# The scaling step of the float64 weight conversion: 60 of 60 on ScalarE in the first feed-forward, where it was 24 of 60

## The chip, the cores and the metric

The kernel runs on one core of one Trainium2 chip. The core has five engines that run side by side, each through its own queue in order: TensorE (PE in the profile; PEld is its weight load), VectorE (DVE), ScalarE (ACT), GpSimd (POOL) and SyncE (SP), which here issues the DMAs. Engines wait for one another by semaphores. The metric is the device time of one execution in microseconds (us), as the median of several runs; lower is better.

## The reference, cut to what matters

```python
x = attention(q, k, v, M_prev, z_prev, beta)   # 4 batches, 8 heads, 576 rows, 64 columns
x = x.reshape(2304, 512)                       # 4 batches of 576 tokens
a = x @ w1                                     # 512 x 1024
b = x @ w2                                     # 512 x 1024
h = a * b @ w3                                 # 1024 x 1024
x = h @ w_out                                  # 1024 x 512
gate = 1 / (1 + exp(-(x @ w_gate)))            # 512 x 1536
val = x @ w_val                                # 512 x 1536
return gate * val @ w_out2                     # 1536 x 512
```

All of attention's inputs are float32. The weights are float64, and the kernel gets them as the bits of 64-bit integers; turning them into float32 is part of the time. The product w3 @ w_out is computed first and once, so that the first feed-forward is (a * b) @ (w3 @ w_out).

## The kernel before, in words

**Stages.** The four batches are worked through one after the other. `ffn(b)` is the feed-forward of batch b, and beside it the attention of batch b + 1 runs in slices that `drive` hands out. Ahead of `ffn(0)` a stage `start()` runs the attention of batch 0 and the first half of w3 @ w_out (PSUM tile `wps`, functions `prep` and `prep_units`). Within a feed-forward PE computes `ab` (x @ w1 and x @ w2, 8 blocks of columns), `xw` (times w3 @ w_out, 4 blocks), `gv` (x @ w_gate and x @ w_val, 12 blocks f = 0 to 11) and `ot` (times the last weight, 4 blocks). Each product is made of three fp32r matmuls, high times high, low times high and high times low, in `prod`, so each weight is split in a high and a low half by `split_rows` (line 311 casts on ACT, line 313 subtracts on DVE or POOL).

**Weights.** Only up to the end of batch 0's feed-forward are weights converted. They come in units of two halves of 128x512 numbers; there are 38 units of float64, so 76 halves. `conv_step` makes a half in three steps, one step a call, and `pump` calls it between the matmuls:

- step 0 scales the upper 32 bits of each number, read as a float32, by 2**-112 into `cy` (lines 198 to 201), scales the lower 32 bits into `cr` on ACT (line 202), and has SP load the half that comes three later (`load64`, line 173, tile `r`, three buffers);
- step 1 shifts `cy` into `wraw` (line 210) and sets the sign (line 211), both on DVE;
- step 2 adds `cr` to it on POOL (line 215).

`cy` and `cr` have two buffers each, `wraw` has three. `split_step` then casts and splits `wraw` into a slot of the ring of five `wslot` tiles, and SP stores the slot to DRAM (line 262, `k`), from where the later batches load it.

**Which engine scales.** Line 198 asks `turn(SHARE_Y)`, which adds up a share for each call and answers yes when the sum passes one. The share is taken by the stage that Python is in when it writes the step: the first number for `start()`, the second for `ffn(0)`, the third for later batches, where no half of float64 is left.

```python
            if turn(SHARE_Y):
                nc.scalar.mul(y, hi, 2.0**-112)
            else:
                nc.vector.tensor_scalar(y, hi, 2.0**-112, None, ALU.mult)
            nc.scalar.activation(out=r, in_=w[:, :, 0].bitcast(U32), func=AF.Copy, scale=2.0**-29)
            load64(conv_rank[s] + R64)
```

**What sets the order.** A list scheduler with a timeline of its own orders each engine's queue; attention's steps get a higher priority in `start()`. From `ffn(0)` on PE's queue stands as it is written; the queues of DVE, ACT, POOL and SP are ordered by the scheduler throughout. So a step on another engine also moves its neighbours.

**Attention's names.** `s` is the PSUM tile of the scores, line 557 takes the scores to `p` on DVE, line 105 (a helper) takes the exponential on ACT, lines 580 and 581 make the factor and line 583 applies it on DVE or POOL; PE then turns `p` round into `t` (line 613). `hgraw` (line 417, DVE) is gate times value and frees the PSUM tiles of `gv`; `gsb` (line 105) is the gate on ACT.

Of the kernel before, what the change touches and what calls it, by code (L numbers as in the profile page):

```python
# [37 lines left out]
SHARE_N = (1.0, 0.5, 0.5)  # L38
SHARE_M = (1.0, 0.3, 0.5)
SHARE_Q = (1.0, 0.5, 0.5)  # L40
SHARE_Y = (1.0, 0.4, 0.0)
SHARE_T = (0.1, 0.0, 0.0)

FRAC = 0.97
# [6 lines left out]
def tile_attention_memory_ffn(  # L51
# [46 lines left out]
    def turn(share):  # L98
        return lower(share) is nc.gpsimd
# [80 lines left out]
    def conv_step():  # L180
# [12 lines left out]
        if ws["step"] == 0:  # L193
# [3 lines left out]
            hi = w[:, :, 1].bitcast(F32)  # L197
            if turn(SHARE_Y):
                nc.scalar.mul(y, hi, 2.0**-112)
# [687 lines left out]
```

## Time and profile before

| | before |
| --- | --- |
| median of 3 runs | 1106.35 us (1105.39 to 1108.88) |
| profiled execution | 1107.55 us |
| its span | 1105.8 us |
| granted TensorE clock over the span | 0.989 |
| busy: PE, PEld | 1063.3 us (96%), 950.7 us (86%) |
| busy: DVE, ACT, POOL | 533.9, 468.7, 326.9 us (48%, 42%, 30%) |

The profiled execution is one run; its span is the time from the first to the last instruction that the profile shows. Matmuls are pipelined, so a PE that is busy all of the time is not PE at its peak. A granted clock of 1.00 is 2.4 GHz and 0.50 is 1.2 GHz.

### The profile page before, as it was taken

The page shows a single profiled execution, that of the slowest core. Times are in us where ns is not written, and L with a number is a line of the kernel's source. Part 1 is how long each engine was busy: PE and PEld are TensorE (multiplying, and loading weights), DVE is VectorE, ACT ScalarE, POOL GpSimd, SP SyncE. Part 2 cuts the span into 40 slices and gives each one's busy share as a digit, 9 for nine tenths or more (in the row PEclk, how much of TensorE's full clock was granted, in tenths as well). Part 3 has the DMA queues.
Part 4 walks back from the last instruction along what each step waited for, and adds up shares of the span by engine and source line. Part 5 has one row for each costly group of instructions (what it writes and reads, how often), then busy time and mean ns, then how long its engine had stood idle before and what let it go on. Part 6 is the DMA issues. An engine that isn't in the chain of part 4 may idle for free.

```text
span 1105.8 us, 19723 instructions
## 1 busy us (share of the span) xinstructions
PE 1063.3 (96%) x7616; PEld 950.7 (86%) x7616; DVE 533.9 (48%) x1251; ACT 468.7 (42%) x1030; POOL 326.9 (30%) x260
## 2 busy tenths in 40 slices
PE   6989798999999899999999999999999999999998
PEld 3555586887999789898999899889999899999998
DVE  7995888758788734553222415544222402212210
ACT  6776565645655633554322424454222412212210
POOL 5887565625666532222000202321000200000000
PEclk9999889999999899999999999999999999999999
DMA  8565568856888556443545454423554355454451
GB/s 271 167 207 186 178 219 287 272 188 211 268 298 305 206 193 220 149 151 128 171 156 171 153 171 159 163 85 134 163 167 160 101 164 189 154 171 171 154 174 61
DMA packets 69238, 201.76 MB, mean 182 GB/s; under 512 B 9624, under 2 KB 15896, under 8 KB 69144
## 3 DMA queue, kind: packets, MB, share of 16 engines
q1 hardware_dynamic: 69144, 200.50, 55.2%
q8 instruction: 60, 0.98, 0.4%
q14 instruction: 34, 0.28, 0.1%
HBM read 160.10 MB, written 40.37 MB: 181 GB/s over the span
## 4 chain that ended last, share of the span: by engine, by line
PE 75%; DVE 13%; POOL 4%; issue 4%; ACT 3%; DMA 2%; SPq 0%; DVEq 0%; POOLq 0%; ACTq 0%
PE gv L302 21%; PE ab L302 18%; PE ot L302 13%; PE xw L302 7%; PE s L552 4%; PE t L613 4%; DVE wraw L211 3%; PE o L681 3%; PE wps L302 3%; DVE wraw L210 2%; POOL wraw L215 2%; DVE p L557 1%; PE o L666 1%; POOL wslot L313 1%; DMA k<-wslot 1%
## 5 line engine op out<-in xcount | busy, mean ns | idle before, releaser
L302 PE MATMUL gv<-x,wslot 128*128 128x288 f32 x2304 | 308.2, 295 | 3.9 <-DVE hgraw L417 2.6
L302 PEld LDWEIGHTS gv<-x,wslot 128*128 128x128 f32 x2304 | 305.8, 188 | 5.8 <-DVE hgraw L417 4.2
L302 PE MATMUL ab<-x,wslot 128*128 128x288 f32 x1536 | 231.7, 303 | 0.0
L302 PEld LDWEIGHTS ab<-x,wslot 128*128 128x128 f32 x1536 | 210.6, 191 | 11.5 <-issue 8.3
L302 PE MATMUL ot<-hg,wslot 128*128 128x288 f32 x1152 | 166.1, 301 | 4.1 <-DVE hg L313 3.8
L583 POOL TENSOR_SCALAR p<-p,sm,omg 116x116 f32<-116x116 f32 (+4 forms) x100 | 100.6, 1010 | 224.2 <-DVE sm L581 159.8
L302 PEld LDWEIGHTS ot<-hg,wslot 128*128 128x128 f32 x1152 | 156.5, 190 | 10.4 <-issue 4.6
L215 POOL TENSOR_TENSOR wraw<-wraw,cr 128x512 int32<-128x512 int32 x76 | 112.1, 1489 | 65.7 <-DVE wraw L211 56.6
L105 ACT ACTIVATE p<-p,sm 116x116 f32<-116x116 f32 (+4 forms) x160 | 92.9, 582 | 73.4 <-DVE sm L557 68.5
L557 DVE CUSTOM_DVE_ANT_0 p<-s,msk 116x116 f32<-116x116 f32 (+4 forms) x160 | 68.2, 453 | 108.5 <-PE s L552 108.3
L417 DVE TENSOR_TENSOR hgraw<-gv,gsb 128x288 f32<-128x288 f32 x96 | 43.7, 455 | 141.5 <-PE gv L302 134.1
L302 PE MATMUL xw<-h,wslot 128*128 128x288 f32 x768 | 111.4, 299 | 0.2 <-DVE h L313 0.2
L302 PEld LDWEIGHTS xw<-h,wslot 128*128 128x128 f32 x768 | 103.1, 188 | 3.8 <-issue 2.5
L105 ACT ACTIVATE gsb<-gv 128x288 f32<-128x288 f32 x96 | 39.4, 410 | 112.0 <-PE gv L302 112.0
L613 PE MATMUL t<-idf,p 116*116 116x116 f32 x480 | 70.1, 276 | 14.0 <-DVE p L583 9.6
L613 PEld LDWEIGHTS t<-idf,p 116*116 116x116 f32 x480 | 54.8, 140 | 28.7 <-issue 16.5
L495 POOL TENSOR_TENSOR me<-mphi,z 116x640 f32<-116x640 f32 x16 | 25.4, 1589 | 176.0 <-issue 174.5
L373 DVE TENSOR_TENSOR hraw<-ab,asb 128x288 f32<-128x288 f32 x64 | 29.1, 456 | 70.1 <-PE ab L302 66.9
L202 ACT ACTIVATE cr<-r 128x512 int32<-128x512 uint32 x76 | 51.4, 676 | 27.0 <-POOL wraw L215 26.9
L211 DVE SCALAR_TENSOR_TENSOR wraw<-cy,wraw 128x512 int32<-128x512 int32 x76 | 62.3, 843 | 0.2
L313 POOL TENSOR_TENSOR wslot<-wraw,wslot 128x512 fp32r<-128x512 f32 x36 | 50.6, 1405 | 29.4 <-ACT wslot L311 28.8
L311 ACT CAST hg<-hgraw 128x576 fp32r<-128x576 f32 x48 | 32.3, 672 | 57.5 <-DVE hgraw L417 57.5
(79 smaller groups left out, 1139.0 us busy)
## 6 DMA issues: line engine op xcount, KB each, us to landing
wslot<-k SPq DMA_DIRECT2D x180, 512.0 KB, 3.6
k<-wslot SPq DMA_DIRECT2D x60, 512.0 KB, 5.6
r<-in_gv_dram SPq DMA_DIRECT2D x24, 512.0 KB, 4.9
qk<-in_qk_dram SPq DMA_DIRECT2D x32, 290.0 KB, 4.1
r<-in_w3t_dram SPq DMA_DIRECT2D x16, 512.0 KB, 4.0
r<-in_w_dram SPq DMA_DIRECT2D x16, 512.0 KB, 4.6
r<-in_o_dram SPq DMA_DIRECT2D x12, 512.0 KB, 5.4
qnr<-in_qn_dram SPq DMA_DIRECT2D x16, 320.0 KB, 3.3
```

What stands on the lines that cost most here:

```text
L105: ins = nc.scalar.activation(**kw)
L202: nc.scalar.activation(out=r, in_=w[:, :, 0].bitcast(U32), func=AF.Copy, scale=2.0**-29)
L211: nc.vector.scalar_tensor_tensor(z, y, -(2**31), z, ALU.bitwise_and, ALU.bitwise_or)
L215: nc.gpsimd.tensor_tensor(z, z, tmp["r"], ALU.add)
L302: nc.tensor.matmul(ps, w[:, wi, blk, :], x[:, xi, cols : cols + n], start=first and part == 0, stop=last and part == 2,)
L313: eng.tensor_sub(dst[:, 1], src, dst[:, 0].bitcast(F32))
L417: nc.vector.tensor_mul(hraw[:, c0 : c0 + HS], pss[1][:, :HS], asb)
L552: nc.tensor.matmul(os_[hh], q_[r, 0, i * T : (i + 1) * T], k_[r, 1, c0:c1], start=x == 0, stop=x == len(terms) - 1,)
L557: nc.vector.tensor_tensor_reduce(out=ps_[hh][:, c0:c1], in0=os_[hh], in1=msk[:, SP - w + c0 : SP - w + c1], scale=-0.125, scalar=3.0e38 if ...
L583: lower(SHARE_N).tensor_scalar(ps_[hh][:, :w], ps_[hh][:, :w], sm[:, 6 + hh : 7 + hh], omg[:T, 2 * p + hh : 2 * p + hh + 1], ALU.mult, ALU ...
L613: nc.tensor.transpose(tp[:T, c : c + T], src[hh][:, j * T : (j + 1) * T], idf[:T, :T])
L681: nc.tensor.matmul(ot[r, XO + q0 : XO + S], v_[:, j, hh], pt[:, hh, j].rearrange("p a c -> p (a c)")[:, q0 - X : S - X] if j < 4 else pt[: ...
```

## The change

One number of a table is given other values. The second one decides: in `ffn(0)` every scaling of the upper bits is put on ACT, where two in five were. The first is as it was, and the third is asked by nobody.

```diff
@@ -38,7 +38,7 @@
 SHARE_N = (1.0, 0.5, 0.5)
 SHARE_M = (1.0, 0.3, 0.5)
 SHARE_Q = (1.0, 0.5, 0.5)
-SHARE_Y = (1.0, 0.4, 0.0)
+SHARE_Y = (1.0, 1.0, 1.0)
 SHARE_T = (0.1, 0.0, 0.0)
 
 FRAC = 0.97
```

In the program, 36 instructions of line 201 leave DVE's queue and 36 of line 199 come to ACT's. No other instruction comes or goes, but the scheduler orders the queues anew, most of all between the end of `start()` and the first `ab` blocks.

The first place is there, on DVE: the attention of batch 1 is at its second and third group of rows (`p_0_1`, `p_0_2`, with the scores `s_0_1`, `s_0_2`), and PE waits for `p_0_1`. This is the queue before, behind the scores `s_0_1`:

```order
L211 SCALAR_TENSOR_TENSOR wraw_1535<-cy_1523,wraw_1535 128x512
L211 SCALAR_TENSOR_TENSOR wraw_1535<-cy_1556,wraw_1535 128x512
L338 TENSOR_TENSOR wpart_1281<-wps_0_1283,wpart_1281 128x512
L201 TENSOR_SCALAR cy_1595<-r_24_1470 128x512
L580 TENSOR_SCALAR sm_0_1_1326<-sm_0_1_1326 116x2
L338 TENSOR_TENSOR wpart_1352<-wps_1_1354,wpart_1352 128x512
L210 TENSOR_SCALAR wraw_1604<-cy_1640 128x512
L210 TENSOR_SCALAR wraw_1604<-cy_1595 128x512
L581 RECIPROCAL sm_0_1_1326<-sm_0_1_1326 116x2
L313 TENSOR_TENSOR wslot_1548<-wraw_1535,wslot_1548 128x512
L557 ISA p_0_2_0_1399,sm_0_2_1401<-s_0_2_0_0_1402,msk 116x348
```

Behind it come the rest of line 557, two of line 211 and then line 583 for `p_0_1`. And this is the queue after, from the scores `s_0_1` on:

```order
L557 ISA p_0_1_1_1325,sm_0_1_1326<-s_0_1_0_1_1328,msk 116x232
L557 ISA sm_0_1_1326 116x1
L313 TENSOR_TENSOR wslot_1457<-wraw_1439,wslot_1457 128x512
L210 TENSOR_SCALAR wraw_1604<-cy_1595 128x512
L338 TENSOR_TENSOR wpart_1281<-wps_0_1283,wpart_1281 128x512
L211 SCALAR_TENSOR_TENSOR wraw_1604<-cy_1595,wraw_1604 128x512
L580 TENSOR_SCALAR sm_0_1_1326<-sm_0_1_1326 116x2
L581 RECIPROCAL sm_0_1_1326<-sm_0_1_1326 116x2
L210 TENSOR_SCALAR wraw_1604<-cy_1640 128x512
L583 TENSOR_SCALAR p_0_1_0_1324<-p_0_1_0_1324,sm_0_1_1326,omg 116x232
L211 SCALAR_TENSOR_TENSOR wraw_1604<-cy_1640,wraw_1604 128x512
L557 ISA p_0_2_0_1399,sm_0_2_1401<-s_0_2_0_0_1402,msk 116x348
```

Line 583 for `p_0_1` stands ahead of the scores `s_0_2` now, and two of line 211 (for `wraw_1535`) have gone ahead of the scores `s_0_1`.

The second place is on ACT in the `gv` blocks of batch 0, here block 2 (before and after in one):

```order
 L311 CAST hg_1_3339<-hgraw_1_3340 128x576
 L105 ACTIVATE gsb_2_0_3451<-gv_2_0_0_3430 128x288
+L199 ACTIVATE cy_3508<-r_62_3375 128x512
 L199 ACTIVATE cy_3549<-r_63_3423 128x512
 L105 ACTIVATE gsb_2_1_3489<-gv_2_1_0_3475 128x288
```

Both scalings of the block stand in front of the second `gsb` now; nothing else moves there, on ACT or on DVE, where line 201 stood between the two `hgraw` of the block.

## Rows read from the trace of the kernel before

**Rows 1.** Busy time by stretch: length, then busy us of PE, PEld, DVE, ACT, POOL, clock, DMA share, GB/s.

```profile
0.00:130.00 130.00, 114.23 (x517) 65.85 (x517) 104.57 (x252) 91.32 (x213) 94.28 (x86) 1.00 0.64 208
130.00:385.00 255.00, 232.27 (x1630) 208.78 (x1631) 201.52 (x400) 151.11 (x311) 148.76 (x106) 0.95 0.73 246
...
430.00:1106.00 676.00, 671.97 (x5132) 635.60 (x5130) 214.15 (x567) 211.52 (x474) 71.08 (x59) 1.00 0.46 151
```

**Rows 2.** Lines 199, 201: durations min/median/max ns, first and last start; ACT's idle time ahead.

```profile
L199 ACT ACTIVATE cy<-r x40: 652/674/699, 7.9 to 376.5; 128x512 f32<-128x512 f32 x40
  DVE wraw L211: 30.2, 14
L201 DVE TENSOR_SCALAR cy<-r x36: 411/1140/1723, 67.8 to 378.1; 128x512 f32<-128x512 f32 x36
```

**Rows 3.** Chain that ended last, 55 to 160 us: start us, us, what.

```profile
67.88 1.65 DVE cy L201
...
132.37 0.81 DVE cy L201
```

**Rows 4.** The same chain, 160 to 285 us, its shares by line.

```profile
by line: PE ab L302 29.2%; PE wps L302 8.9%; issue 8.1%; DVE wraw L211 6.3%; PE s L552 5.3%; PE t L613 5.2%; PE o L681 3.9%; DVE cy L201 3.3%; DVE wslot L313 2.9%; DVE wraw L210 2.6%; POOL wraw L215 2.3%; DVE p L557 2.2%; PE o L666 1.8%; AC
```

**Rows 5.** Timeline, DVE at 130 us: start us, us, engine, line, operation, tiles, count.

```profile
130.17 0.39 DVE L557 CUSTOM_DVE_ANT_0 p<-s,msk 116x232 f32<-116x232 f32 x1
...
130.49 1.28 DVE L211 SCALAR_TENSOR_TENSOR wraw<-cy,wraw 128x512 int32<-128x512 int32 x2
...
132.30 0.89 DVE L201 TENSOR_SCALAR cy<-r 128x512 f32<-128x512 f32 x1
...
134.25 0.68 DVE L338 TENSOR_TENSOR wpart<-wps,wpart 128x512 f32<-128x512 f32 x1
...
135.59 0.67 DVE L313 TENSOR_TENSOR wslot<-wraw,wslot 128x512 fp32r<-128x512 f32 x1
136.18 0.51 DVE L557 CUSTOM_DVE_ANT_0 p<-s,msk 116x348 f32<-116x348 f32 x1
...
137.06 1.28 DVE L211 SCALAR_TENSOR_TENSOR wraw<-cy,wraw 128x512 int32<-128x512 int32 x2
138.27 1.33 DVE L583 TENSOR_SCALAR p<-p,sm,omg 116x232 f32<-116x232 f32 x1
```

**Rows 6.** Timeline, PE, same place, with idle time ahead; then busy time by stretch.

```profile
139.75 1.00 PE L613 MATMUL t<-idf,p 116*116 116x116 f32 x4 [7.64 <-DVE p L583]
...
131.61:145.26 13.65, 6.01 (x27) 5.69 (x26) 12.12 (x25) 6.57 (x13) 9.59 (x7) 0.50 0.68 198
```

**Rows 7.** Timeline, the first `hgraw` of blocks 0 and 11 of `gv`.

```profile
290.55 0.45 DVE L417 TENSOR_TENSOR hgraw<-gv,gsb 128x288 f32<-128x288 f32 x1
...
367.51 0.45 DVE L417 TENSOR_TENSOR hgraw<-gv,gsb 128x288 f32<-128x288 f32 x1
```

**Rows 8.** Timeline of one block of `gv`, POOL and DVE.

```profile
332.27 3.02 POOL L215 TENSOR_TENSOR wraw<-wraw,cr 128x512 int32<-128x512 int32 x2 [2.23 <-DVE wraw L211]
335.24 1.30 POOL L313 TENSOR_TENSOR wslot<-wraw,wslot 128x512 fp32r<-128x512 f32 x1
...
332.98 1.14 DVE L201 TENSOR_SCALAR cy<-r 128x512 f32<-128x512 f32 x1
...
335.32 1.76 DVE L313 TENSOR_TENSOR wslot<-wraw,wslot 128x512 fp32r<-128x512 f32 x1 [0.83 <-ACT wslot L311]
```

**Rows 9.** Timeline, POOL, at a place where DVE was idle as POOL began.

```profile
144.04 2.52 POOL L215 TENSOR_TENSOR wraw<-wraw,cr 128x512 int32<-128x512 int32 x2
```

**Rows 10.** Timeline, ACT and SP, from one block's first `cr` to the next one's.

```profile
334.11 0.67 ACT L202 ACTIVATE cr<-r 128x512 int32<-128x512 uint32 x1
...
334.81 1.54 SPq L173 DMA_DIRECT2D r<-in_o_dram  x2
...
340.03 0.68 ACT L199 ACTIVATE cy<-r 128x512 f32<-128x512 f32 x1 [3.17 <-DVE hgraw L417]
...
341.41 0.67 ACT L202 ACTIVATE cr<-r 128x512 int32<-128x512 uint32 x1
```

## The prediction, made before the changed kernel ran

> **What bounds the kernel now.** I read the busy times by stretch first [rows 1]. From 430 us on PE is busy 671.97 of 676 us at a clock of 1.00, and no weight is converted there any more: that part is PE's own and the change doesn't touch it. What can move lies ahead of it. From 0 to 130 us PE is idle 15.8 us, from 130 to 385 us 22.7 us, at a mean clock of 0.95. In both stretches DVE is the busiest of the other engines (104.57 of 130 us, 201.52 of 255 us), ACT the one with more room (91.32 and 151.11 us). So I asked next what the 36 scalings cost DVE [rows 2], whether they are on the chain of work that ended last [rows 3, 4], what PE waits for in its longest stop [rows 5, 6], and what sets the pace of the `gv` blocks, which stand beside the last conversions [rows 7 to 10].
>
> **The change part by part.**
>
> *The work itself.* DVE loses 36 scalings, ACT gets 36 of 0.674 us, that is 24.3 us [rows 2]. On DVE one takes 0.411 us at best but 1.140 us in the median and up to 1.723 us: its time is not its own, it stands still until POOL's instruction is done (in the `gv` block it begins at 332.98, and ends at 334.12, just after POOL's first line 215, which began at 332.27 and took half of 3.02 us [rows 8]). On ACT the spread is 0.652 to 0.699 us.
>
> The Trainium skill speaks against the change: "ScalarE: Activation LUTs", Rules for kernel authors, tells to put a multiplication on VectorE and not on ScalarE. By the shortest durations here that would hold (0.411 against 0.652 us), by the medians it doesn't. By that rule the two front terms of the sum below would be nothing, and the time that of the first rival.
>
> *55 to 160 us.* On the chain the scaling at 67.88 us stands with 1.65 us [rows 3], in a stretch where DVE works without a gap. Its substitute on ACT is 0.67 us, beside a DVE that is late anyway. I take the 1.65 us off, rounded to **-1.6 us**; the ends are 0 (ACT is late in its place) and -1.65.
>
> *PE's stop at 132 to 140 us.* PE waits 7.64 us for line 583 on `p_0_1` [rows 6]. Behind the scores `s_0_1` at 130.17 us DVE does eight microseconds of other things before it comes to that line at 138.27 us [rows 5]. The new order, shown above, puts behind line 583: the scores `s_0_2` (136.18 to 137.06, 0.88 us), one line 211 (half of 1.28, 0.64), one line 338 (0.68) and one line 313 (0.67); and the scaling at 132.30 us (0.89, on the chain with 0.81 [rows 3]) goes. That is 3.76 us. Against it: on ACT the two exponentials that line 580 needs now stand behind a second scaling and a `cr` that waits for POOL, and the partner of `p_0_1` on POOL stands behind three of line 215. I take half, **-2.0 us**; the ends are 0 and -3.8. The clock is a part of its own: it was at 0.50 from 131.61 to 145.26 us [rows 6], so from PE's resumption at 139.75 to 145.26 us PE did in 5.5 us what takes 2.75 us at 1.00. A shorter stop may give that back; a shorter stop may also bring the same fall. I take 0, and keep -2.75 as the end.
>
> *160 to 285 us.* The scalings have 3.3% of this chain [rows 4], of 125 us 4.1 us. The larger part of that chain is PE's own, and for each piece removed the next in line may be POOL's line 215 or a cast. I take half, **-2.0 us**; ends 0 and -4.1.
>
> *The twelve `gv` blocks, 290 to 368 us.* From block 0 to block 11 they take 76.96 us [rows 7], 7.00 us each. Two loops are near that length. The first goes through POOL: two of line 215 (3.02 us), the split on POOL (1.30), then DVE's split, which is held until POOL ends (1.76 from 335.32 [rows 8]), then lines 210, 313 and 211 and POOL again. Line 215 alone takes 2.52 us for two [rows 9]; of the 0.50 us more I give half to the scaling and half to line 211, which also falls in it. So this loop would fall by 0.25 us a block, 12 x 0.25 = 3.0 us. The second loop goes through ACT and the loads: the first `cr` of a block at 334.11 us frees a buffer, SP loads at 334.81, the scaling on ACT waits for it until 340.03, `gsb` and a cast stand behind it, and the next `cr` comes at 341.41: 7.30 us [rows 10]. Before, most blocks had one of their scalings on DVE, so ACT didn't wait for the load; after the change both stand in front of `gsb` in every block. At 7.30 us a block that would cost 12 x 0.30 = 3.6 us. How long a load takes decides between the two. I take the middle, rounded to **0 us**, with -3.0 and +3.6 as the ends.
>
> The first of the two scalings costs ACT nothing there, since it can run while ACT now waits: 30.2 us of ACT's idle time ended with line 211, 14 times, ahead of a scaling [rows 2].
>
> "GPSIMD Engine Reference", Specifications, in the Trainium skill says that GpSimd shares its memory interfaces with VectorE, and that they contend with VectorE's two-port modes or instructions with two memory inputs. The trace agrees: 3.02 us against 2.52 us [rows 8, 9].
>
> **Sum.** -1.6 - 2.0 - 2.0 + 0 = -5.6 us. Against the profiled execution's 1107.55 us (a span of 1105.8 us and 1.75 us around it) that is 1101.95 us. That execution is 1.2 us over the median of the runs, so on the median of 1106.35 us it is 1100.75 us. I forecast **1101 us**, 0.5% faster. A measurement of this kernel can tell about 0.3%, 3.3 us, from no change, so the border is at 1103.0 us and the other one at 1109.7 us.
>
> **The rivals.**
>
> *The scalings' places on the chain are taken by others* (no change). For it: PE and POOL hold most of the chain from 160 us on [rows 4], and each scaling that moves still has to be done before line 210 can run, now behind ACT's casts and exponentials. Against it: at 132 us the queue itself becomes shorter in front of what PE waits for. Only the 1.6 us at 68 us would be left: 1106.35 - 1.6 = 1104.75, say 1105 us.
>
> *ACT is held by its loads* (slower). The second loop above binds in all blocks: +3.6 us. The same queue order, scaling, then what PE or DVE waits for, then `cr`, holds for the 18 units that are converted in `ffn(0)` ahead of or behind those 12; at 0.30 us in half of them 2.7 us more, with nothing won at the front. 1106.35 + 6.3 = 1112.7 us. It decides itself by the time from a load's issue to the scaling: 5.22 us in the block shown (334.81 to 340.03 [rows 10]); at about 4.9 us the loop is as long as the blocks were, 7.00 us, and above that it costs.
>
> *POOL freed and the clock kept* (faster by more). All ends of the sum on the good side: 1.65 + 3.8 + 2.75 + 4.1 + 3.0 = 15.3 us, 1091 us; with the `gv` blocks' 3.0 and the clock's 2.75 alone on top of the forecast 1095 us.
>
> That the change doesn't do what it says is no rival: the queues show 36 instructions gone from one engine and 36 come to the other.
>
> **How the numbers follow.** The forecast has 0.48 (its own range 1097 to 1104 us, of which 0.05 lies within 0.3%); the first rival 0.22, the second 0.20, the third 0.10. Faster by over 0.3%: 0.43 + 0.10 = 0.53. Within: 0.22 + 0.05 = 0.27. Slower: 0.20. The range goes from the best end, 1091 us, to 1112 us, which leaves out the upper half of the slower rival (0.10) and a little of the third (0.03).
>
> **What would show it.** Right: PE's wait for line 583 near 132 us at 6 us or less; the two of line 215 in a `gv` block at about 2.8 us; DVE's busy time down by some 40 us (36 of the median's 1.14), ACT's up by 24 us; the first `hgraw` of the `gv` blocks 6.75 to 7.3 us apart, and the mean of the twelve tells which loop won. Wrong: ACT idle ahead of a scaling with a load as its releaser in most blocks, and blocks of 7.2 us or more (second rival); the stop at 132 us as long as before or another one like it, with another fall of the clock (then the front terms are lost); PE not busy throughout from 430 us on (then I have looked at the wrong part).

## The result, and the profile after

The changed kernel takes 1094.82 us in the median of four runs (1093.54 to 1096.02), the kernel before 1106.24 us beside it: a ratio of 0.989, with an interval of 0.987 to 0.991. That is 11.4 us less, on the side that I forecast and inside the range, but over twice the 5.35 us of the forecast. The profiled execution of after is its fastest run (1093.54 us, a span of 1091.6 us), that of before lies above its median; between the two spans there are 14.2 us. What follows divides those 14.2 us.

The page of after, first its engines, then the groups of lines 215, 199 and 211 over the whole run (busy us, mean ns of one, idle time ahead and what ended it):

```profile
PE 1059.9 (97%) x7616; PEld 947.9 (87%) x7616; DVE 506.6 (46%) x1215; ACT 486.9 (45%) x1066; POOL 319.7 (29%) x260
...
L215 POOL TENSOR_TENSOR wraw<-wraw,cr 128x512 int32<-128x512 int32 x76 | 109.9, 1458 | 66.5 <-DVE wraw L211 60.6
...
L199 ACT ACTIVATE cy<-r 128x512 f32<-128x512 f32 x76 | 50.6, 675 | 50.6 <-issue 27.9
...
L211 DVE SCALAR_TENSOR_TENSOR wraw<-cy,wraw 128x512 int32<-128x512 int32 x76 | 66.6, 898 | 0.2
```

To see where the time came from I cut both traces at three points of the computation: PE's second `ab` product, its first `gv` product and its first `ot` product. The stretches hold the same matmuls in both kernels. Busy time by stretch of before (length, then busy us of PE, PEld, DVE, ACT, POOL, clock, DMA share, GB/s):

```profile
0.00:144.88 144.88, 121.17 (x548) 72.10 (x549) 118.30 (x281) 98.94 (x230) 103.85 (x93) 0.95 0.64 206
144.88:285.12 140.24, 133.40 (x947) 113.55 (x947) 108.13 (x243) 83.02 (x181) 75.58 (x58) 0.99 0.70 236
285.12:368.01 82.89, 78.70 (x578) 76.53 (x576) 68.08 (x111) 48.84 (x93) 52.68 (x36) 1.00 0.88 294
```

And of after:

```profile
0.00:136.37 136.37, 120.26 (x549) 71.09 (x549) 113.33 (x270) 101.98 (x237) 101.16 (x91) 0.97 0.66 213
136.37:270.50 134.13, 130.56 (x948) 111.63 (x946) 103.97 (x235) 89.05 (x193) 75.76 (x59) 1.00 0.75 251
270.50:354.28 83.78, 79.17 (x578) 76.61 (x576) 52.88 (x96) 56.64 (x108) 48.33 (x36) 1.00 0.85 286
```

The **front** became 8.5 us shorter (144.88 to 136.37), the **middle** 6.1 us (140.24 to 134.13), the **gv blocks** 0.9 us longer (82.89 to 83.78); the rest of the run differs by 0.5 us. In the front PE's idle time (length less busy) fell from 23.7 to 16.1 us, and its busy time by 0.9 us. In the middle idle time fell from 6.8 to 3.6 us, and PE's busy time by 2.8 us at a clock of 1.00 instead of 0.99.

PE's long stop in the front [rows 6] has gone. PE in after at the same place (start, us, idle time ahead in brackets):

```profile
122.08 0.27 PE L552 MATMUL s<-qkl,qkh 64*116 64x232 f32 x2
123.94 0.73 PE L302 MATMUL wps<-wo,wslot 128*128 128x512 f32 x2 [1.60 <-ACT wo L311]
126.30 0.80 PE L302 MATMUL wps<-wo,wslot 128*128 128x512 f32 x1 [1.62 <-POOL wo L313]
...
133.59 0.56 PE L613 MATMUL t<-idf,p 116*116 116x116 f32 x4
```

The transposition of `p_0_1`, which began at 139.75 us after a wait of 7.64 us [rows 6], begins at 133.59 us without one. Before had a second stop there, and handed the scores `s_0_1` over at 124.3 us:

```profile
124.05 0.27 PE L552 MATMUL s<-qkl,qkh 64*116 64x232 f32 x2
...
130.30 0.73 PE L552 MATMUL s<-qkh 64*116 64x348 f32 x2 [1.72 <-DVE sm L557]
```

In place of these two stops (1.72 and 7.64 us) after has two earlier ones of 3.2 us in all.

### The profile page after: what moved, and what is told of

Same layout as the page of the kernel before. It is cut to its first block, busy times and chain, and to the rows that moved or that the text cites. A ratio compares the mean times of both kernels' runs of the same rounds, so it can differ in the third digit from the quotient of the medians.

```text
span 1091.6 us, 19687 instructions
## 1 busy us (share of the span) xinstructions
PE 1059.9 (97%) x7616; PEld 947.9 (87%) x7616; DVE 506.6 (46%) x1215; ACT 486.9 (45%) x1066; POOL 319.7 (29%) x260
## 4 chain that ended last, share of the span: by engine, by line
PE 65%; DVE 1%; DMA 1%; ACT 1%; issue 0%; POOL 0%; ACTq 0%; POOLq 0%
PE gv L302 21%; PE ab L302 15%; PE ot L302 13%; PE xw L302 7%; PE s L552 3%; PE t L613 2%; PE o L681 2%; PE o L666 1%; DMA k<-wslot 1%; PE o L674 1%; DMA r<-in_o_dram 0%; PE qt L650 0%; DVE wraw L210 0%; DVE wslot L313 0%; DVE p L557 0%
## 5 line engine op out<-in xcount | busy, mean ns | idle before, releaser
L302 PE MATMUL ab<-x,wslot 128*128 128x288 f32 x1536 | 227.8, 300 | 0.0
L302 PEld LDWEIGHTS ab<-x,wslot 128*128 128x128 f32 x1536 | 207.0, 188 | 11.2 <-issue 8.2
L302 PEld LDWEIGHTS ot<-hg,wslot 128*128 128x128 f32 x1152 | 156.5, 190 | 10.1 <-issue 4.6
L583 POOL TENSOR_SCALAR p<-p,sm,omg 116x116 f32<-116x116 f32 (+4 forms) x100 | 97.7, 980 | 213.0 <-DVE sm L581 137.3
L215 POOL TENSOR_TENSOR wraw<-wraw,cr 128x512 int32<-128x512 int32 x76 | 109.9, 1458 | 66.5 <-DVE wraw L211 60.6
L199 ACT ACTIVATE cy<-r 128x512 f32<-128x512 f32 x76 | 50.6, 675 | 50.6 <-issue 27.9
L211 DVE SCALAR_TENSOR_TENSOR wraw<-cy,wraw 128x512 int32<-128x512 int32 x76 | 66.6, 898 | 0.2
L313 POOL TENSOR_TENSOR wslot<-wraw,wslot 128x512 fp32r<-128x512 f32 x36 | 47.9, 1330 | 35.2 <-ACT wslot L311 35.0
```

The lines of the kernel that those rows point to most:

```text
L211: nc.vector.scalar_tensor_tensor(z, y, -(2**31), z, ALU.bitwise_and, ALU.bitwise_or)
L215: nc.gpsimd.tensor_tensor(z, z, tmp["r"], ALU.add)
L302: nc.tensor.matmul(ps, w[:, wi, blk, :], x[:, xi, cols : cols + n], start=first and part == 0, stop=last and part == 2,)
L313: eng.tensor_sub(dst[:, 1], src, dst[:, 0].bitcast(F32))
L583: lower(SHARE_N).tensor_scalar(ps_[hh][:, :w], ps_[hh][:, :w], sm[:, 6 + hh : 7 + hh], omg[:T, 2 * p + hh : 2 * p + hh + 1], ALU.mult, ALU ...
```

## Experiments

The line numbers of some kernels differ by up to three from those of the program above. The kernels with the scratch tile `cz` also drop a tile that nothing reads (`idr`), with its one copy on ScalarE at the start, to make room. All ratios are to the kernel before, with 95% intervals.

**The change in three parts.** Each kernel is before with one third of the scalings moved. The front's third:

```diff
-            if turn(SHARE_Y):
+            if turn(SHARE_Y) or s < 30:
```

> Only the first third of the change: the 9 DVE scalings of the half units below 30 (the last at about 146 us) go to ACT, the later 27 stay on DVE. Theory 'each stretch pays for itself' (the lag of the matmuls of after against before grows by 7.4 us up to 145 us, and by 7.2 us from there to 285 us): 7.4 us faster than before, about 1099 us, with the stop for line 583 near 133 us and its fall of the clock to 0.50 as in after (6.8 us long instead of 13.7), and the later falls and stops of before (at about 200 us) still there. Theory 'all of it starts at the front' (PE ahead at 145 us meets the later work in another phase and so loses the later stops too): 13 us faster, about 1094 us, as after. Theory 'the places on the chain are taken by others' (first rival): 1105 us.

1101.28 us, 0.9948 (0.993 to 0.997). The middle third:

```diff
-            if turn(SHARE_Y):
+            if turn(SHARE_Y) or 30 <= s < 58:
```

> Only the middle third: the 12 DVE scalings of half units 30 to 57 (155 to 292 us) go to ACT, those ahead and behind stay on DVE. Theory 'each stretch pays for itself': the stop at 132 to 140 us as before, then 6 to 7 us gained between 160 and 285 us, among them the fall of the clock at 206.7 us; about 1099.5 us. Theory 'all of it starts at the front': 0 to -2 us, 1104 to 1106 us. My forecast's own term for this stretch was -2.0 us with -4.1 as its end: 1104 us, 1102 at best.

1101.43 us, 0.9952 (0.994 to 0.996). The last third:

```diff
-            if turn(SHARE_Y):
+            if turn(SHARE_Y) or s >= 58:
```

> Only the last third: the 15 DVE scalings of half units from 58 on (the gv blocks and the units of the output projection) go to ACT. By the lag of after against before (from -14.6 us at gv block 0 to -13.5 us at the end): 1 us slower than before, about 1107 us, blocks 7.00 to 7.05 us apart, ACT waiting for a load ahead of the scaling in most blocks. If POOL's freed time counted alone: 3 us faster, 1103 us, blocks of 6.75 us. If ACT's loop through the loads binds in full: 3.6 us slower, 1110 us, blocks of 7.30 us.

1107.9 us, 1.0013 (1.0002 to 1.0025). In us that is -5.5, -5.3 and +1.2 (the `gv` blocks of the last third's trace are 7.13 us apart): each stretch pays for itself, and the sum of the medians, -9.6 us, is near the whole, within the intervals. First the same two stretches in the trace of the front's third, then in that of the middle third:

```profile
0.00:137.70 137.70, 119.25 (x548) 70.42 (x549) 112.63 (x270) 102.30 (x237) 101.08 (x91) 0.93 0.64 211
137.70:279.94 142.24, 134.62 (x948) 114.61 (x946) 111.28 (x246) 84.09 (x183) 78.26 (x59) 0.98 0.70 237
```

```profile
0.00:145.86 145.86, 121.42 (x548) 72.55 (x549) 118.47 (x281) 99.44 (x231) 101.94 (x93) 0.89 0.62 204
145.86:279.81 133.95, 131.12 (x946) 111.71 (x946) 102.45 (x233) 87.73 (x191) 73.13 (x57) 1.00 0.72 247
```

Moving the front's nine gains 7.2 us there and gives 2.0 us back in the middle, where no scaling moved (its clock falls to 0.50 twice there, for 3.41 us each, before's once); moving the middle's twelve leaves the front about as it was (1.0 us longer, see the last section) and gains 6.3 us in the middle.

**VectorE's work put back.** A shorter queue on VectorE was my reason. So VectorE gets its work back, while ScalarE's result is used:

```diff
-            if turn(SHARE_Y):
+            if not turn(SHARE_Y):
+                cz = fp.tile([128, 512], F32, tag="cz", name=f"cz{s}", bufs=1)
+                nc.vector.tensor_scalar(cz, hi, 2.0**-112, None, ALU.mult)
+            if True:
```

> The changed kernel with VectorE's work put back: all scalings are done on ScalarE and used from there, and VectorE does the 36 that it lost once more into a scratch tile that nobody reads (a tile that no work needs is dropped for its room). Theory 'VectorE's time is what pays' (its queue, with POOL's holds in it): the gain is lost, 1104 to 1108 us, with the long stop ahead of line 583 near 132 us. Theory 'the chain from the load through the scaling pays' (ACT has the result in 0.67 us where DVE's stands in its queue): the gain stays, 1095 to 1098 us.

1104.57 us, 0.998 (0.997 to 0.999), between the two theories, and the stretches say why:

```profile
0.00:135.91 135.91, 116.38 (x548) 69.22 (x549) 117.44 (x275) 101.74 (x236) 103.04 (x91) 0.95 0.65 214
135.91:278.42 142.51, 134.99 (x948) 114.56 (x946) 111.00 (x251) 89.10 (x194) 76.25 (x59) 0.96 0.69 237
278.42:364.98 86.56, 80.02 (x579) 76.81 (x577) 64.53 (x110) 57.25 (x108) 50.27 (x36) 1.00 0.85 279
```

The front keeps its whole gain (135.91 us), the middle loses all of it (142.51), the gv blocks are 3.7 us longer than before's. So the front's gain is not VectorE's time. The reverse puts work on ScalarE and takes none from VectorE:

```diff
-            if turn(SHARE_Y):
+            on_act = turn(SHARE_Y)
+            if not on_act:
+                cz = fp.tile([128, 512], F32, tag="cz", name=f"cz{s}", bufs=1)
+                nc.scalar.mul(cz, hi, 2.0**-112)
+            if on_act:
```

> The kernel before, and ScalarE does the 36 scalings that VectorE does once more, into a scratch tile that nobody reads (a tile that no work needs is dropped for its room): the cost of the change on ScalarE's side alone, 36 x 0.67 = 24.3 us of its time, with nothing taken from VectorE. Theory 'ScalarE has room': 0 ahead of 285 us and up to +2 us in the gv blocks from waits for loads, 1106 to 1108.5 us. Rival 'ScalarE's time costs as VectorE's does': half of the 9.6 us that the moves gained or more, 1111 us or above.

1112.94 us, 1.0053 (1.004 to 1.007). By its total the rival won; by its stretches neither was right. The front is nearly as short as after's, although VectorE does all of its 36. The middle is 4.8 us longer than before's, with three falls of the clock where before has one; what of that is ScalarE's added work was not taken apart. The gv blocks pay 9.1 us: ScalarE waits 33.4 us for loads there, where before's profile names none, most of it ahead of the copies. That each copy also holds its load buffer longer fits this, but was not tested by itself (busy time by stretch):

```profile
0.00:137.19 137.19, 121.17 (x548) 71.36 (x549) 118.30 (x276) 100.71 (x234) 101.36 (x91) 0.98 0.66 213
137.19:282.27 145.08, 136.37 (x948) 116.16 (x946) 110.41 (x249) 89.11 (x195) 76.83 (x58) 0.96 0.69 229
282.27:374.28 92.01, 79.84 (x576) 76.76 (x577) 67.81 (x112) 56.67 (x110) 53.10 (x37) 1.00 0.82 267
```

ScalarE's two longest waits in the gv blocks, in us in total, times, longest:

```profile
ACT cz L200 <- DMA r<-in_gv_dram: 14.7, 7, 5.3
ACT cz L200 <- DMA r<-in_o_dram: 9.7, 5, 2.7
```

**Is the front's gain the order's?** Both of these kernels, and the front's third, have line 583 for `p_0_1` ahead of the scores `s_0_2` in VectorE's queue, as after has. The scheduler set that order from its own estimate of when each input is ready. First one piece of it alone: in the kernel before, VectorE's scores `s_0_2` are bound behind line 583 (the line that binds; two more only give the two instructions their names).

```diff
+                if (b, p, i) in UP: tc.add_manual_dep(ttr.ins, last[b, p, i - 1, True].ins.name, mybir.DependencyInfo(mybir.DependencyClass.NoSync, mybir.DependencyReason.DATA), reason="order")
```

> The kernel before with one piece of VectorE's order changed and no work moved: in the second batch the scores s_0_2 (line 557, 0.88 us) may only issue behind line 583 for p_0_1. Theory 'what stands in the queue ahead of line 583 sets PE's stop': the stop at 132 us falls from 7.6 to about 6.7 us, and the time by 0.9 us, 1105.5 us. Rival 'the stop is set by something else ahead (the exponentials or POOL's half)': no change, stop 7.2 to 7.6 us, 1106.5 us. If the order alone made the front's gain of the change: 1101 us.

1105.61 us, 0.9986 (0.9974 to 0.9998). PE's wait fell by 1.69 us, twice what I expected:

```profile
139.34 1.00 PE L614 MATMUL t<-idf,p 116*116 116x116 f32 x4 [5.95 <-DVE p L584]
```

The 0.88 us of the scores went as expected, and line 583 itself (584 here) took 0.45 us where it had taken 1.33 us [rows 5], since POOL's instruction beside it was now near its end (last section). Then nearly the whole order of the change, with no work taken from VectorE: ScalarE does the nine scalings of the front as well, for nobody.

```diff
-            if turn(SHARE_Y):
+            on_act = turn(SHARE_Y)
+            if not on_act and s < 30:
+                cz = fp.tile([128, 512], F32, tag="cz", name=f"cz{s}", bufs=1)
+                nc.scalar.mul(cz, hi, 2.0**-112)
+            if on_act:
```

> The kernel before, in which ScalarE also does the 9 scalings of VectorE below half unit 30, into a scratch tile that nobody reads; VectorE still does all of its own 36 and these are the ones used (a tile that no work needs is dropped for its room). VectorE loses nothing, but the orders of the queues up to 146 us become nearly those of the change, with line 583 for p_0_1 ahead of the scores s_0_2. Theory 'the front's gain comes from the order': as p1_front, 4 to 7 us faster than before, 1100 to 1103 us, and PE idle about 11.5 us up to its second ab block instead of 18.8. Theory 'it comes from VectorE's time': 1106 us or more, and the stop ahead of line 583 as before.

1101.51 us, 0.9955 (0.994 to 0.997): the same as the front's third, which moves these nine (1101.28 us). The front's stretch:

```profile
0.00:137.55 137.55, 121.77 (x549) 71.49 (x549) 117.86 (x276) 100.70 (x234) 101.43 (x91) 0.98 0.64 212
```

So in the front the order is worth 7.3 us in the trace (5.9 us in the medians), and the freed time of VectorE, given that order, nothing that these runs can tell. The other traces agree: the front takes 135.9 to 138.5 us in the six with the new order, 143.9 to 147.3 us in the six without it, the kernel with one bound piece among them. Which part of the order does it was not taken apart; it is the order of all queues up to there, PE's own too.

**Is the middle's gain VectorE's time?** The middle third changes nothing in PE's order, though the scheduler reorders the other engines' queues there as well. VectorE does its twelve scalings there once more, ScalarE's are used:

```diff
-            if turn(SHARE_Y):
+            on_act = turn(SHARE_Y)
+            if not on_act and 30 <= s < 58:
+                cz = fp.tile([128, 512], F32, tag="cz", name=f"cz{s}", bufs=1)
+                nc.vector.tensor_scalar(cz, hi, 2.0**-112, None, ALU.mult)
+            if on_act or 30 <= s < 58:
                 nc.scalar.mul(y, hi, 2.0**-112)
```

> The middle third alone (p2_mid: the 12 scalings from 155 to 292 us on ScalarE), with VectorE's work put back: VectorE does those 12 once more into a scratch tile that nobody reads. PE's order is the same as before and as in p2_mid. Theory 'in the middle VectorE's time is what pays': the gain of p2_mid (5.3 us) is lost, 1105 to 1107 us, with PE idle 6 to 7 us between its second ab block and the first gv block. Theory 'the scaling's place on the way of a weight pays, not VectorE's time': 1101 to 1102 us, idle 2.2 us as in p2_mid.

1110.0 us, 1.0033 (1.002 to 1.005): the gain is gone, and 2.6 us beyond. What PE waited for in the middle, first in the middle third, then with the work put back (us in total, times, longest):

```profile
PE s L552 <- DVE sm L557: 1.1, 1, 1.1
...
PE t L613 <- DVE p L583: 0.4, 1, 0.4
```

```profile
PE t L616 <- DVE p L586: 4.1, 1, 4.1
PE s L555 <- DVE sm L560: 3.3, 2, 2.3
```

The waits that come and go are those for VectorE's scores and softmax scaling. But the copies do not only take VectorE's time: VectorE also stood idle 9.4 us ahead of them for their loads, where before it stood 2.1 us ahead of its scalings. The longest wait, 4.1 us where before has 1.91 us at this place, has such an idle time ahead of it, VectorE's row first, then PE's:

```profile
176.35 1.16 DVE L200 TENSOR_SCALAR cz<-r 128x512 f32<-128x512 f32 x1 [2.79 <-DMA r<-in_w_dram]
...
180.74 0.57 PE L616 MATMUL t<-idf,p 116*116 116x116 f32 x2 [4.09 <-DVE p L586]
```

That is the likely reason for the 2.6 us beyond. So in the middle it is VectorE's queue that pays: the stretch takes 133.9 to 134.1 us in the three traces in which VectorE is relieved there (after, the middle third, and the first two thirds below), and 140.1 to 145.1 us in the eight in which it does the twelve or copies of them (the last kernel of this section, which changes the loads too, is left out). How much of that is VectorE's busy time and how much its new order is not shown, since no run holds VectorE's order there.

**Versions that might beat both.** The first two thirds without the last (the condition is `s < 58`):

> The first two thirds of the change without the last: all scalings of the half units below 58 on ScalarE, the 15 behind them (the gv blocks and the output projection) stay on VectorE, as before. Theory 'the parts add up and the last third costs' (p1 -5.5, p2 -5.3, p3 +1.4 us against before, the whole change -11.4): between -10.8 (the parts' sum) and -12.8 us (the whole less the last third), 1093.5 to 1096 us, gv blocks 7.00 us apart, not slower than the whole change. Rival 'the last third gains once the front is fast': above 1097 us.

1095.5 us, 0.9889 (0.987 to 0.991), no different from the whole change. The last third costs so little that it can stay or go. Then the load loop of the gv blocks: both results are written back into the load buffer, and five such buffers replace three (the diff is against the changed kernel).

```diff
-R64 = 3
+R64 = 5
-            y = fp.tile([128, 512], F32, tag="cy", name=f"cy{s}", bufs=2)
-            r = fp.tile([128, 512], I32, tag="cr", name=f"cr{s}", bufs=2)
+            y, r = hi, w[:, :, 0]
```

> The changed kernel in which both halves of a number are written back into the buffer that they were loaded to (no cy and cr), and the room goes into five load buffers instead of three. Theory 'in the gv blocks ACT waits for its loads': no scaling waits for a load there, blocks 6.75 us apart as those of the changed kernel with a quick load, 3 us faster than the changed kernel, about 1092 us. Rival 'the operands with a stride cost DVE and POOL as much, or a buffer that is held to the end of the conversion loads no earlier': 1095 us or more, blocks of 7.0 us or more.

1120.36 us, 1.0116 (1.010 to 1.014): a miss. The group of the scaling in this kernel, over the whole run:

```profile
L198 ACT ACTIVATE r<-r 128x512 f32<-128x512 f32 x76 | 51.5, 677 | 57.4 <-DMA r<-in_gv_dram 25.2 <-DMA r<-in_o_dram 12.6 <-DMA r<-in_w_dram 8.3
```

The stride costs little (677 ns against 675, and the others are within 5% of after). The scaling now waits 46 us for the loads in this row, where after's profile names loads for 8.4 us (and nothing for 27.9 us). In the gv blocks a load is issued only when POOL has added (the DMA queue's waits there are for line 214, this kernel's line 215), no longer when ScalarE is done. The gv blocks are 5.9 us longer than after's, but the front is 10.9 and the middle 10.1 us longer, and what of this is the loads' and what the order's was not taken apart. The front keeps an old-style order here, with the scores `s_0_2` ahead of line 583, and PE's stops there are 4.64 and 4.51 us although VectorE is relieved.

## Why the prediction came out as it did

**55 to 160 us, -1.6 us: size right by luck, reason wrong.** PE's stop near 79 us, 1.56 us long, is gone in after. It ended with an instruction of ScalarE (`qts`), and it is gone just as well where VectorE keeps all its scalings (the kernel of the front's order). PE's own queue changed here: two scores that stood behind the waiting transposition now stand ahead of it, before first, then after:

```profile
80.41 0.48 PE L613 MATMUL t<-idf,p 116*116 116x116 f32 x3 [1.56 <-ACT qts L646]
80.82 0.74 PE L552 MATMUL s<-qk 64*116 64x290 f32 x2
...
78.70 0.74 PE L552 MATMUL s<-qk 64*116 64x290 f32 x2
79.37 0.51 PE L613 MATMUL t<-idf,p 116*116 116x116 f32 x3
```

It was the order, not the 1.65 us on the chain [rows 3].

**The stop at 132 us, -2.0 us: mechanism half right, size wrong.** I looked for what stands behind the scores `s_0_1` in the queue and counted 3.76 us. I began at 130.17 us [rows 5], when VectorE came to these scores. PE had delivered them at 124.3 us. Ahead of them, VectorE in before did this:

```profile
124.66 0.41 DVE L201 TENSOR_SCALAR cy<-r 128x512 f32<-128x512 f32 x1
125.00 1.91 DVE L504 TENSOR_TENSOR mphi<-mphi,mn 116x640 f32<-116x640 f32 x1
126.83 0.75 DVE L313 TENSOR_TENSOR x<-o,x 128x576 fp32r<-128x576 f32 x1
127.50 1.83 DVE L210 TENSOR_SCALAR wraw<-cy 128x512 int32<-128x512 int32 x2
129.25 0.68 DVE L313 TENSOR_TENSOR wslot<-wraw,wslot 128x512 fp32r<-128x512 f32 x1
129.85 0.39 DVE L557 CUSTOM_DVE_ANT_0 p<-s,msk 116x232 f32<-116x232 f32 x1
```

In after the scores come 2.7 us after PE's, and line 583 soon behind:

```profile
125.03 0.39 DVE L557 CUSTOM_DVE_ANT_0 p<-s,msk 116x232 f32<-116x232 f32 x1
...
129.94 1.36 DVE L583 TENSOR_SCALAR p<-p,sm,omg 116x232 f32<-116x232 f32 x1
```

From PE's scores to the end of line 583 it was 15.3 us before and is 9.0 us now, 6.3 us less, of which the two scalings in it (0.41 and 0.89 us) are 1.3. Of the 6.3 us, 3.5 lie behind the moment at which VectorE came to the scores, near the 3.76 us that I counted, and 2.8 ahead of it, which I did not look at. The step that failed is the place at which the comparison of the two queues began, and the halving of what it found. PE's stops there fell by 6.1 us net (9.36 to 3.22), more than my end of 3.8. What I took the half off for, late exponentials and POOL's late part of `p_0_1`, made PE wait for nothing here; ScalarE and POOL cost 3.2 us at another place, the stops for `wo`.

**The clock, 0 us: nearly right in the front.** It was at 0.50 for 13.65 us before, most of that idle, and for 6.83 us in after, most of that busy; PE's busy time differs by 0.9 us there. In the middle, where the sum had no term for it, the fall of 3.4 us behind the stop at 205 us is gone.

**160 to 285 us, -2.0 us: wrong, and beyond its end.** The middle gave 6.1 us. I had taken the scaling's own share of the chain, 4.1 us [rows 4], as all that it could give. But the scalings in this stretch took 11.9 us of VectorE's time, as its group in the middle of before shows:

```profile
L201 DVE TENSOR_SCALAR cy<-r 128x512 f32<-128x512 f32 x13 | 11.9, 919 | 2.1 <-DMA r<-in_w3t_dram 2.0
```

The step that failed is to take the share as the upper end. The gain lies between the two figures, and with the work put back it was all lost again (with the loads' waits on top, as said above). What is queued behind a scaling is late with it, and stands on the chain under its own line; that is the likely reason, beside the new order of VectorE's queue. The clock's fall came on top: at half the clock 3.4 us cost an estimated 1.7 us of the 6.1.

The rule of the Trainium skill that I set against the change ("ScalarE: Activation LUTs", Rules for kernel authors: a multiplication belongs on VectorE) fares so: in the front, moving the work indeed gave nothing beyond its order; in the middle these runs go against it, 6.3 us for twelve moved multiplications. The prediction has a slip here: with both front terms at nothing its sum leaves the 2.0 us of the middle, while the first rival leaves 1.6 us of the front.

**The gv blocks, 0 us: size right.** They are 7.04 us apart in the mean of eleven (first `hgraw` at 276.35, last at 353.78 us), against 7.00 [rows 7]. The term was the middle between two loops, and which of them sets the pace is still open. Line 215's pair takes 2.83 us instead of 3.02 [rows 8], as described. A load is named ahead of five of the scalings only (5.8 us in all); ahead of eleven, 18.5 us, the profile names nothing that ScalarE waited for. So the sign that I gave for the loop of the loads, a load as the releaser in most blocks, did not show. In one block of after:

```profile
317.66 2.83 POOL L215 TENSOR_TENSOR wraw<-wraw,cr 128x512 int32<-128x512 int32 x2 [2.66 <-DVE wraw L211]
...
318.80 0.67 ACT L199 ACTIVATE cy<-r 128x512 f32<-128x512 f32 x1 [0.55 <-DMA r<-in_gv_dram]
```

"GPSIMD Engine Reference", Specifications, in the Trainium skill (GpSimd and VectorE contend for shared memory interfaces) agrees with that pair's 0.19 us, which is small. I had expected 0.25, half of the 0.50 us between rows 8 and rows 9. But line 215 was not alone in [rows 9]; a scaling began beside the second of the two, and the pair took 2.52 us all the same:

```profile
145.75 1.10 DVE L201 TENSOR_SCALAR cy<-r 128x512 f32<-128x512 f32 x1 [2.02 <-DMA r<-in_w3t_dram]
```

**VectorE's busy time** fell by 27 us, not 40. The scalings had 37.2 us, but what held them holds others now: line 211 went from 843 to 898 ns a piece. ScalarE's rose by 18 us, not 24.

Of the rivals, the first (1105 us) and the second (1112.7 us) didn't come. The third had the right sum, not the right terms: neither POOL nor the clock made it, but the order in the front and VectorE's queue in the middle. Why the scheduler's new order is the better one stays open: it follows from its estimates, and nothing in the change aims at it.

## What to carry to other kernels

Where a scheduler sets the order, moving work between engines is two changes at once: run the new order with the old work (an idle copy on the new engine) and the old work put back (an idle copy on the old engine), or the gain is credited to the wrong one. See that the copy waits for nothing that the old work did not wait for. When pricing a stop, begin at the moment at which the waiting engine handed its result over, and count everything that the other engine does from there, ahead of the consumer as well as behind it. On an engine that is late all along, take the moved work's share of the chain as no upper end: here the gain, 6.1 us, lay between that share (4.1 us) and the work's full time in the queue (11.9 us). And check whether the engine that takes it also holds a load buffer longer.

## What the runs showed that I had not expected

The first 40 us differ between the traces, probably from execution to execution: in four of them (the front's third, the middle third, VectorE's work put back, the one piece of the order) PE waits 3.6 us for scores near 36 us, with a clock of 0.50 behind it, where before has 0.93 us, and no moved scaling lies ahead of that place. PE came there earlier, since its matmuls ahead ran faster (two scores took 0.84 us at 33.51 us in the middle third, 1.51 us at 33.44 us in before, both at a granted clock of 1.00); why stays open. In the middle third:

```profile
39.44 1.12 PE L552 MATMUL s<-qk 64*116 64x464 f32 x1 [3.61 <-DVE sm L557]
```

Two of these four profiles (the front's third, VectorE's work put back) still reach their second `ab` product 7 to 9 us before that of before, so it doesn't make the front's gain; it adds to the noise of a single trace.

One instruction of VectorE (line 583, 116 rows of 232 numbers) took 0.45 or 1.33 us, by how long POOL's instruction beside it still ran. At 1.33 us [rows 5] it ended 0.14 us behind the first of two of POOL's line 215, which in before began at 137.89 us and took half of 2.84 us:

```profile
137.89 2.84 POOL L215 TENSOR_TENSOR wraw<-wraw,cr 128x512 int32<-128x512 int32 x2 [1.22 <-DVE wraw L211]
```

With the scores bound behind it, it met POOL's own half of the softmax scaling shortly before that ended, and ended 0.13 us behind it, first POOL's row, then VectorE's:

```profile
137.20 1.86 POOL L584 TENSOR_SCALAR p<-p,sm,omg 116x232 f32<-116x232 f32 x1 [1.54 <-DVE sm L582]
...
138.74 0.45 DVE L584 TENSOR_SCALAR p<-p,sm,omg 116x232 f32<-116x232 f32 x1
```

The scalings on VectorE show the same: 29 of before's 36 end 0.28 or 0.29 us behind an instruction of POOL, and take 0.67 to 1.72 us; the other seven take 0.41 to 0.43 us.
